# Keys, values and queries of one layer in half-array products, with another PSUM layout and batched sums

## The chip, the cores and the metric

The kernel runs on one core of a Trainium2 chip. The metric is device time in microseconds of one launch. Matrix products run on TensorE (PE in the profile, its weight loads PEld), elementwise work on VectorE (DVE), ScalarE (ACT) and GpSimd (POOL); SyncE (SP) issues the DMA transfers. Products are collected in PSUM, which the kernel lays out in banks of 512 float32 values per partition: four in the pool `ps_h` and two for each of the two tags of `ps_acc`.

## The reference

Four layers run one after the other on x of 2048 tokens by 576 channels: linear attention (A), MLP (B), attention again, MLP again. Layers 1 and 3 share their weights, and so do 2 and 4.

```python
def _A_ref(x, wqkv, wo):
    H = 32; Dh = D // H                       # 32 heads of 18
    q, k, v = ...                             # from x @ wqkv, 576 -> 3 * 576
    phi = lambda t: jnp.where(t > 0, t + 1, jnp.exp(t)) + 1e-6
    pq, pk = phi(q), phi(k)
    kv = jnp.einsum("bhsd,bhse->bhde", pk, v) # sum over all tokens
    z = jnp.einsum("bhsd->bhd", pk)
    num = jnp.einsum("bhqd,bhde->bhqe", pq, kv)
    den = jnp.einsum("bhqd,bhd->bhq", pq, z)[..., None] + 1e-6
    o = num / den
    return o... @ wo

def _B_ref(x, w1, b1, w2, b2):
    h = _gelu(layernorm(x) @ w1 + b1)         # 576 -> 4608
    return h @ w2 + b2

x = x + _A_ref(_layernorm(x), A_wqkv, A_wo)
x = x + _B_ref(_layernorm(x), ...)
x = x + _A_ref(_layernorm(x), A_wqkv, A_wo)   # Layer 3, the one that changes
x = x + _B_ref(_layernorm(x), ...)
```

## The kernel before

Tokens are cut into 16 tiles of 128 (`t`), and into four blocks of 512 (`c`). The normalized rows are held turned, as `yT`: channels on the partitions in five blocks of 128 (`KD`), tokens along the row. 576 channels are four and a half blocks, so the fifth block holds channels in its upper 64 partitions; the lower 64 partitions of the weights' fifth block are zero in `wqkv_sb`.

`layer_A` makes keys, values and queries. For each token tile `k_proj` (L443) makes two halves of 288 key columns, each of five products of the full array in one bank of the pool `ps_h` (four banks, tag "h"). `v_proj` (L456) makes two value parts of 252 and 324 columns in the two banks of `v_ps` (pool `ps_acc`, tag "accB"). From the third tile on, `q_proj` (L491) makes one group of up to 126 query columns for 512 tokens, five products of 512 columns, again in `ps_h`. The feature map phi is `phi_from_psum` (exponential and shifted copy on ACT, minimum and maximum on DVE) for queries and the first key half, and `phi_by_dve` (exponential on ACT; minimum L376 and a sum that reads PSUM, L378, on DVE) for the second key half. Values are copied to one of two tiles `v_ring`, four groups by ACT (L475) and the fifth by DVE (L480). `kv_acc(t - 1)` (L483) then adds the tile's five products into `kvacc` (pool `ps_acc`, tag "accA"), which stays open over all 16 tiles.

The order of PE's instructions is the order in which they are written: `pe` chains them. Each other engine runs its own instructions in the order in which they stand, and waits on semaphores. At the start of Layer 3 the layer norms of the last two row tiles are still under way: the residual sum of the last MLP tile (L427), the turning of rows (L230), statistics (L296 to L306), the power on POOL (L315) and the normalization (L334), all but the power on DVE. `pre_a1(t)` ticks that pipe once per tile. `land` brings a block of turned rows from DRAM to `yT` by two transfers, three for an MLP.

The MLP's first product (`m1_group`, L653) already works with half arrays: rows 0 to 63 and rows 64 to 127 of the array take separate products of 64 channels, with 4 or 5 products of 512 columns for each of four output blocks per half. The code lets the two halves take turns on a PSUM bank, and a relay stands between them: a tiny ACT copy (L699) that waits for the last product of one half and that the first product of the other half waits for.

After the last tile come `kvT`, the denominators, `kv_wo` and `wo_stage`, which use `ps_h` and both tags of `ps_acc`.

Of the kernel before, what the change touches and what calls it, by code (L numbers as in the profile page):

```python
# [15 lines left out]
P = 128  # L16
# [18 lines left out]
def build(tc, A_x, A_wqkv, A_wo, B_w1, B_b1, B_w2, B_b2, out, dbg=None, n_layers=4):  # L35
    nc = tc.nc
    dbg = dbg or {}
    with ExitStack() as ctx:
        const = ctx.enter_context(tc.tile_pool(name="const", bufs=1))
        ps_h = ctx.enter_context(tc.tile_pool(name="ps_h", bufs=4, space=PSUM))  # L40
        ps_acc = ctx.enter_context(tc.tile_pool(name="ps_acc", bufs=1, space=PSUM))
        dpool = ctx.enter_context(tc.tile_pool(name="dram", bufs=1, space=DRAM))

        x_in = A_x.flatten_outer_dims()
# [84 lines left out]
        relay_sb = const.tile([P, 2], F32, name="relay_sb")  # L129
        nc.gpsimd.memset(relay_sb[:], 0.0)  # L130
        chain = dict(last=None)

# [131 lines left out]
        class LNPipe:  # L264
            def __init__(self):
                self.items = []
# [94 lines left out]
            def drain(self):  # L361
                while self.items or landing:
                    self.tick()
# [9 lines left out]
        def phi_by_dve(ps_ap, out_ap, rows, n):  # L373
            e = work.tile([P, 512], BF16, name="phi_e", bufs=3)
            act_last["exp"] = nc.scalar.activation(out=e[0:rows, 0:n], in_=ps_ap, func=ACT.Exp).ins.name
            nc.vector.tensor_scalar(out=e[0:rows, 0:n], in0=e[0:rows, 0:n], scalar1=1.0, scalar2=1e-6,  # L376
                                    op0=ALU.min, op1=ALU.add)
            top = nc.vector.scalar_tensor_tensor(out=out_ap, in0=ps_ap, scalar=C1, in1=e[0:rows, 0:n],  # L378
                                                 op0=ALU.add, op1=ALU.max)
            dve_last["phi"] = top.ins.name  # L380

        def phi_from_psum(ps_ap, out_ap, rows, n, turned_cols=False):
            e = work.tile([P, 512], BF16, name="phi_e", bufs=3)
            a = work.tile([P, 512], BF16, name="phi_a", bufs=2)
            e_out, a_out = e[0:rows, 0:n], a[0:rows, 0:n]
            if turned_cols:
                e_out, a_out, ps_ap = spread(e_out), spread(a_out), gather(ps_ap)
            act_last["exp"] = nc.scalar.activation(out=e_out, in_=ps_ap, func=ACT.Exp).ins.name  # L388
            act_last["phi"] = nc.scalar.activation(out=a_out, in_=ps_ap, func=ACT.Identity, bias=C1,
                                                   scale=1.0).ins.name  # L390
            nc.vector.tensor_scalar(out=e[0:rows, 0:n], in0=e[0:rows, 0:n], scalar1=1.0, scalar2=1e-6,  # L391
                                    op0=ALU.min, op1=ALU.add)
            top = nc.vector.tensor_tensor(out=out_ap, in0=a[0:rows, 0:n], in1=e[0:rows, 0:n], op=ALU.max)
            dve_last["phi"] = top.ins.name
# [40 lines left out]
            return xn  # L435

        def layer_A(li, next_kind, pre_a1=None):
            kvacc = ps_acc.tile([P, 2, 512], F32, name="kvacc", tag="accA")
            pk_tiles = {}
            v_tiles = {}  # L440
            pq = {}
# [41 lines left out]
            def kv_acc(t):  # L483
                pk = pk_tiles.pop(t)
                va = v_tiles.pop(t)
                for g in range(G):
                    dst = kvacc[:, 0, GO[g]:GO[g] + GR[g]] if g < 4 else kvacc[:, 1, 0:GR[g]]
                    pe(nc.tensor.matmul(dst, lhsT=va[:, g, :], rhs=pk[:, GO[g]:GO[g] + GR[g]],  # L488
                                     start=(t == 0 and g in (0, 4)), stop=(t == NT - 1), skip_group_check=True))

            def q_proj(g, c):  # L491
# [5 lines left out]
                pq[(g, c)] = blk.tile([P, D], BF16, name="pq", tag="blk")  # L497
                phi_from_psum(qp[0:GR[g], :], pq[(g, c)][0:GR[g], 0:CA], GR[g], CA, turned_cols=(li > 0))

            q_left = [(g, c) for c in range(NCA) for g in range(G)]  # L500
            pe_chain["on"] = True
            for t in range(NT):
                if t != 1 or li > 0:
                    k_proj(t)
                if t == 0 and li == 0:
# [10 lines left out]
            q_proj(*q_left.pop(0))  # L516

            nc.vector.tensor_tensor(
                out=kvT[0:127, 0:4, :].rearrange("p g (h e) -> p g h e", h=7),
                in0=kvacc[0:127, 0, 0:504].rearrange("p (g h e) -> p g h e", g=4, h=7),  # L520
# [124 lines left out]
        class LayerB:  # L645
# [69 lines left out]

            def run(self):
                li, next_kind = self.li, self.next_kind

                def feed_next(c, i):
                    if c + 1 < NCB:  # L720
                        t = (c + 1) * TPC + i
                        lnp.feed(None, t, "B", "dve", "dma", load_from=t, after=dve_last["sum"])

                for c in range(NCB):
                    for g in range(self.done.get(c, 0), NGRP):
                        self.m1_group(c, g)
                        if g in (3, 5):
                            prefetch_xo(li, c * TPC + (g - 3) // 2, add_b2=True)
                        if g in (2, 3, 4, 5):
                            feed_next(c, g - 2)  # L730
                        lnp.tick(transposes=0)
                        lnp.tick(transposes=0)
                    self.flush()
                    if c == NCB - 1 and next_kind == "A":
                        warm_table(ACT.Exp, act_last["gelu"])
                    hT = self.hT.pop(c)
                    for j in range(TPC):
                        t = c * TPC + j
                        acc = ps_acc.tile([P, 2, 512], F32, name="m2_ps", tag=next_acc())
                        by_half = li == n_layers - 1 and t == NT - 1  # L740
                        steps = [(f, half) for half in range(2) for f in range(NF)] if by_half else \
                            [(f, half) for f in range(NF) for half in range(2)]
                        for f, half in steps:
                            pe(nc.tensor.matmul(acc[:, half, 0:HALF], lhsT=hT[f][:, j * P:(j + 1) * P],  # L744
                                                rhs=w2_sb[:, f, half * HALF:(half + 1) * HALF],
                                                start=(f == 0), stop=(f == NF - 1)))
# [113 lines left out]
```

## Time and profile before

| | |
|---|---|
| time, median of 3 runs (lowest to highest) | 777.58 us (777.58 to 777.61) |
| the profiled execution's own time | 777.09 us |
| its span | 775.4 us |
| PE busy | 765.1 us |
| DVE, ACT, POOL busy | 277.7, 335.1, 120.5 us |
| k_ps products of the full array (L449), Layers 1 and 3 | 320, 286 ns each |
| q_ps products (L494) | 200, 382 ns each |
| half-array products of 64x512 (L694) | 2592, 376 ns each |
| granted TensorE clock | 1.00 |

The duration of a product runs from its start to the end of its last write; products follow each other faster than that, since they are pipelined. In the profile `h_ps` and `hp_ps` are the two kinds of PSUM tile of the MLP's first product, `m_ps` that of its second, `w_sb` and `w_tail` its weights. Row tiles in DRAM are `x_d` and `y_d`.

### The profile page before, as it was taken

How to read it: one execution, taken by the hardware profiler on the slowest of the kernel's cores; microseconds unless marked ns; L12 is line 12 of the kernel's file. 1: busy time of each engine (PE TensorE's matmuls, PEld its weight loads, DVE VectorE, ACT ScalarE, POOL GpSimd, SP SyncE). 2: the span in 40 equal slices, each digit the busy share in tenths (PEclk: the TensorE clock that was granted, in tenths of full speed). 3: DMA queues.
4: the chain of work that ended last, by engine and by line, in shares of the span. 5: the costliest groups of instructions: out<-in, count | busy, mean ns of one | idle time of the engine just before them, and what ended most of it. 6: DMA issues, size and time to landing. Idle time of an engine off the chain costs nothing.

```text
span 775.4 us, 15774 instructions
## 1 busy us (share of the span) xinstructions
PE 765.1 (99%) x6613; PEld 495.0 (64%) x6613; DVE 277.7 (36%) x714; ACT 335.1 (43%) x734; POOL 120.5 (16%) x185
## 2 busy tenths in 40 slices
PE   8999999999999999999999999999999999999998
PEld 5776664675477457646777766547745764675476
DVE  7786964046013503401355579520140032000000
ACT  5888646404610650264046675561065026305600
POOL 4671322012000301200100004110030011001000
PEclk9999999999999999999999999999999999999999
DMA  8991474016301810320440006630141033011000
GB/s 254 267 299 46 137 253 103 18 50 173 88 16 48 199 50 32 92 64 17 138 107 1 1 2 210 248 82 8 32 129 52 16 124 80 8 32 54 1 11 21
DMA packets 73761, 69.10 MB, mean 89 GB/s; under 512 B 34266, under 2 KB 58330, under 8 KB 73690
## 3 DMA queue, kind: packets, MB, share of 16 engines
q1 hardware_dynamic: 73690, 68.10, 30.0%
q8 instruction: 51, 0.84, 0.5%
q14 instruction: 20, 0.16, 0.1%
HBM read 45.67 MB, written 22.41 MB: 88 GB/s over the span
## 4 chain that ended last, share of the span: by engine, by line
PE 94%; DVE 4%; issue 1%; ACT 1%; DMA 0%; POOL 0%; DVEq 0%; ACTq 0%
PE m_ps L744 37%; PE h_ps L694 20%; PE hp_ps L694 16%; PE q_ps L494 5%; PE k_ps L449 5%; PE wo_ps L589 4%; PE v_ps L470 3%; PE v_ps L462 2%; PE kvacc L488 1%; PE tp L352 1%; PE rden_ps L578 1%; PE warm_ps L176 1%; DVE rden L564 1%; DVE xo L427 0%; DMA x_d<-xo 0%
## 5 line engine op out<-in xcount | busy, mean ns | idle before, releaser
L744 PE MATMUL m_ps<-w_sb,hT 128*128 128x288 bf16 x2304 | 283.6, 286 | 0.0
L744 PEld LDWEIGHTS <-hT 128*128 128x128 bf16 x2304 | 224.8, 98 | 59.8 <-issue 3.4
L694 PEld LDWEIGHTS <-w_sb 64*128 64x128 bf16 x2304 | 124.5, 94 | 136.5 <-issue 1.9
L694 PE MATMUL hp_ps<-yT,w_sb 64*128 64x512 bf16 x1152 | 178.0, 376 | 0.0
L694 PE MATMUL h_ps<-yT,w_sb 64*128 64x512 bf16 x1152 | 148.0, 376 | 0.0
L699 ACT COPY relay_sb<-relay_sb 128x1 f32<-128x1 f32 x144 | 28.6, 198 | 264.5 <-PE h_ps L694 222.2
L315 POOL TENSOR_TENSOR ln_rstd<-ln_u,neg_half 128x1 f32<-128x1 f32 x64 | 36.8, 577 | 480.4 <-DVE ln_u L306 239.7
L690 ACT ACTIVATE hT<-h_ps,b1T 128x512 bf16<-128x512 f32 x144 | 91.2, 684 | 44.4 <-PE h_ps L694 44.4
L690 ACT ACTIVATE hT<-hp_ps,b1T 128x512 bf16<-128x512 f32 x144 | 91.2, 693 | 0.0
L427 DVE TENSOR_TENSOR xbf<-m_ps,xo 128x576 bf16<-128x576 f32 (+1 forms) x17 | 12.2, 722 | 219.9 <-PE m_ps L744 219.9
L427 DVE TENSOR_TENSOR xo<-m_ps,xo 128x576 f32<-128x576 f32 x16 | 12.1, 758 | 179.2 <-PE m_ps L744 179.2
L411 POOL TENSOR_TENSOR xo<-xo,b_bc 128x576 f32<-128x576 f32 x32 | 40.9, 1284 | 102.5 <-DMA xo<-x_d 62.7
L694 PE MATMUL h_ps<-yT,w_tail 64*128 64x512 bf16 x144 | 54.1, 376 | 0.0
L694 PE MATMUL hp_ps<-yT,w_tail 64*128 64x512 bf16 x144 | 54.1, 376 | 0.0
L494 PE MATMUL q_ps<-yT,wqkv_sb 128*126 128x512 bf16 (+1 forms) x200 | 50.0, 382 | 0.0
L589 PE MATMUL wo_ps<-kvwo,pq 126*128 126x288 bf16 (+1 forms) x320 | 43.9, 285 | 1.7 <-DVE pq L581 0.7
L449 PE MATMUL k_ps<-wqkv_sb,yT 128*128 128x288 bf16 x320 | 44.3, 286 | 0.0
L589 PEld LDWEIGHTS <-pq 126*128 126x128 bf16 (+1 forms) x320 | 30.2, 97 | 13.1 <-DVE pq L581 1.8
L449 PEld LDWEIGHTS <-yT 128*128 128x128 bf16 x320 | 31.0, 98 | 11.4
L694 PEld LDWEIGHTS <-w_tail 64*128 64x128 bf16 x288 | 27.1, 94 | 17.1
L388 ACT ACTIVATE phi_e<-k_ps 128x288 bf16<-128x288 f32 x46 | 19.3, 419 | 34.6 <-PE k_ps L449 33.6
L391 DVE TENSOR_SCALAR phi_e<-phi_e 128x288 bf16<-128x288 bf16 (+2 forms) x86 | 25.1, 292 | 24.6 <-ACT phi_e L388 24.5
(100 smaller groups left out, 633.2 us busy)
## 6 DMA issues: line engine op xcount, KB each, us to landing
xo<-x_d SPq DMA_DIRECT2D x48, 288.0 KB, 3.6
x_d<-xo SPq DMA_DIRECT2D x32, 288.0 KB, 2.1
xl<-x_d SPq DMA_DIRECT2D x24, 288.0 KB, 4.6
y_d<-turned SPq DMA_DIRECT2D x40, 144.0 KB, 3.2
w_sb<-in_B_w_dram SPq DMA_DIRECT2D x6, 864.0 KB, 9.5
yT<-y_d SPq DMA_DIRECT2D x10, 512.0 KB, 4.1
w_sb<-in_B_w_dram SPq DMA_DIRECT2D x9, 512.0 KB, 5.6
x_d<-xn SPq DMA_DIRECT2D x16, 288.0 KB, 2.2
```

Source lines behind the costliest of these rows:

```text
L315: nc.gpsimd.tensor_tensor(out=rstd[:], in0=it["u"][:], in1=neg_half[:], op=ALU.pow)
L391: nc.vector.tensor_scalar(out=e[0:rows, 0:n], in0=e[0:rows, 0:n], scalar1=1.0, scalar2=1e-6, op0=ALU.min, op1=ALU.add)
L411: nc.gpsimd.tensor_tensor(out=xo[:], in0=xo[:], in1=b2_bc[:], op=ALU.add)
L427: total = nc.vector.tensor_tensor(out=xn[:, cols].rearrange("p (h n) -> p h n", h=nh), in0=ps, in1=xo[:, cols].rearrange("p (h n) -> p h n ...
L449: pe(nc.tensor.matmul(kp[:, 0:HALF], lhsT=yT[:, k, tok], rhs=wqkv_sb[:, k, D + half * HALF: D + (half + 1) * HALF], start=(k == 0), stop=( ...
L470: pe(nc.tensor.matmul(vp[:, 1, 0:324], lhsT=yT[:, k, tok], rhs=wqkv_sb[:, k, 2 * D + 252: 3 * D], start=(k == 0), stop=(k == KD - 1)))
L494: pe(nc.tensor.matmul(qp[0:GR[g], :], lhsT=wqkv_sb[:, k, GO[g]:GO[g] + GR[g]], rhs=yT[:, k, c * CA:(c + 1) * CA], start=(k == 0), stop=(k ...
L589: pe(nc.tensor.matmul(wp[:, half, 0:HALF], lhsT=pq[(g, c)][0:GR[g], j * P:(j + 1) * P], rhs=kvwo[g][0:GR[g], half * HALF:(half + 1) * HALF ...
L690: act_last["gelu"] = nc.scalar.activation(out=to, in_=ps, func=ACT.Gelu_apprx_tanh, bias=b1T[:, f:f + 1], scale=1.0).ins.name
L694: mm = pe(nc.tensor.matmul(dst[n], lhsT=wt, rhs=mv, start=(seen[n] == 0), stop=(seen[n] == 8)))
L699: relay = nc.scalar.copy(out=relay_sb[:, 1:2], in_=relay_sb[:, 0:1])
L744: pe(nc.tensor.matmul(acc[:, half, 0:HALF], lhsT=hT[f][:, j * P:(j + 1) * P], rhs=w2_sb[:, f, half * HALF:(half + 1) * HALF], start=(f == ...
```

## The change

Layer 3 (`li > 0`) gets a loop of its own; Layer 1 keeps the old one.

Each value part, key half and query group becomes a job (`half_jobs`, `q_job`) of 64-row products: four for each half of the array, and one more for one of them (`tail`), which takes the last 64 channels. `RowTiles` writes the order. Jobs enter the upper half as they come; a job enters the lower half when two later ones have been added. Products are written in the order in which two counters of columns say that they would start. Between a job's last upper product and its first lower one stands a relay, here a POOL memset on `relay_sb`. So that keys and values may take their tail in the lower half, the last 64 rows of the weights are loaded a second time to partitions 64 to 127 (one transfer, at the start of the MLP before), and `land` loads the last 64 channels of `yT` to both halves for Layer 3 too.

The jobs of a tile stand in the order query, values, keys, where the old loop had keys, values, sums, query. Both key halves go by `phi_by_dve`. The PSUM pool `ps_acc` is closed at the start of the layer, and two new ones take its place: `v_banks` with two single banks for the value parts, and `ps_kv` for `kvacc`. Behind `kvT` they are closed and `ps_acc` is opened again. The sums of four tiles are written together, after tiles 4, 8 and 12 and at the end, with the full array; for that the value ring grows to five tiles by the three `y_ring` tiles, each prepared by three POOL memsets. The pipe of layer norms is ticked twice per tile.

```diff
-        ps_acc = ctx.enter_context(tc.tile_pool(name="ps_acc", bufs=1, space=PSUM))
+        psum_pools = ctx.enter_context(ExitStack())
+        ps_acc = psum_pools.enter_context(tc.tile_pool(name="ps_acc", bufs=1, space=PSUM))
...
-                for hi in range(2 if kind == "B" else 1):
+                for hi in range(2):
...
+                def v_start(half):
+                    def start():
+                        tiles[half] = v_banks.tile([P, 512], F32, name="v_ps", tag="v")[:, 0:edges[half + 1] - edges[half]]
...
+                def v_finish(half):
+                    def finish():
+                        nc.scalar.copy(out=va[:, 2 * half:2 * half + 2, 0:126],
+                                       in_=tiles[half][:, 0:252].rearrange("p (g c) -> p g c", g=2))
+                        if half == 1:
+                            nc.vector.tensor_copy(out=va[:, 4, 0:72], in_=tiles[1][:, 252:324])
...
+                def k_finish(half):
+                    def finish():
+                        phi_by_dve(tiles["k", half], tiles["pk"][:, half * HALF:(half + 1) * HALF], P, HALF)
...
+                for half in range(2):
+                    cols = slice(2 * D + edges[half], 2 * D + edges[half + 1])
+                    jobs.append(dict(w=y_of, m=rows_of(cols), tail=1, n=edges[half + 1] - edges[half],
+                                     start=v_start(half), finish=v_finish(half)))
+                for half in range(2):
+                    cols = slice(D + half * HALF, D + (half + 1) * HALF)
+                    jobs.append(dict(w=y_of, m=rows_of(cols), tail=1 - half, n=HALF,
+                                     start=k_start(half), finish=k_finish(half)))
...
+            class RowTiles:
...
+                def emit(self, op, first, last):
+                    job, hi, w, m = op
+                    mm = pe(nc.tensor.matmul(job["dst"], lhsT=w, rhs=m, start=(first and hi == 0), stop=(last and hi == 1)))
+                    self.at[hi] += job["n"]
+                    if first and hi == 1:
+                        tc.add_manual_dep(mm.ins, job["relay"], SYNC, reason="row tiles take turns on a PSUM bank")
+                    if last and hi == 0:
+                        relay = nc.gpsimd.memset(relay_sb[:, 2:3], 0.0)
+                        tc.add_manual_dep(relay.ins, mm.ins.name, SYNC, reason="row tiles take turns on a PSUM bank")
+                        job["relay"] = self.relay = relay.ins.name
+                    if last and hi == 1:
+                        job["finish"]()
+
+                def lower(self, limit):
+                    while self.low and (limit is None or self.at[1] <= limit):
+                        self.emit(*self.low.pop(0))
...
+                def add(self, job):
+                    if len(self.begun) == 2:
+                        if not self.low:
+                            self.at[1] = max(self.at)
+                        self.queue_lower(self.begun.pop(0))
+                    self.begun.append(job)
+                    job["dst"] = job["start"]()
+                    ops = self.ops(job, 0)
+                    for i, op in enumerate(ops):
+                        self.lower(self.at[0] - 1)
+                        self.emit(op, i == 0, i == len(ops) - 1)
+
+                def full(self, func):
+                    func()
+                    self.at = [max(self.at)] * 2
...
+            if li > 0:
+                va_ring = v_ring + [y[:].rearrange("p (g c) -> p g c", g=G) for y in
+                                    (y_ring[(state["ycnt"] + i) % NY] for i in range(NY))]
+                psum_pools.close()
+                v_banks = psum_pools.enter_context(tc.tile_pool(name="v_banks", bufs=2, space=PSUM))
+                ps_acc = psum_pools.enter_context(tc.tile_pool(name="ps_kv", bufs=1, space=PSUM))
+                stream = RowTiles()
+                for t in range(NT):
+                    pre_a1(t)
+                    pre_a1(t)
+                    if t in (2, 3, 4):
...
+                    if t >= 2:
+                        stream.add(q_job(*q_left.pop(0)))
+                    for job in half_jobs(t):
+                        stream.add(job)
+                    if t % 4 == 0 and t > 0:
+                        stream.full(lambda: [kv_acc(u) for u in range(t - 4, t)])
+                stream.drain()
+                for u in range(NT - 4, NT - 1):
+                    kv_acc(u)
...
+            if li > 0:
+                psum_pools.close()
+                ps_acc = psum_pools.enter_context(tc.tile_pool(name="ps_acc", bufs=1, space=PSUM))
...
+                if next_kind == "A":
+                    nc.sync.dma_start(out=wqkv_sb[64:P, 4, D:3 * D], in_=A_wqkv[4 * P:D, D:3 * D])
```

More of the change, by code (lines that the diff above doesn't have):

```diff
@@ L128, in build @@
         SYNC = mybir.DependencyInfo(mybir.DependencyClass.Sync, mybir.DependencyReason.DATA)
-        relay_sb = const.tile([P, 2], F32, name="relay_sb")
+        relay_sb = const.tile([P, 4], F32, name="relay_sb")
         nc.gpsimd.memset(relay_sb[:], 0.0)
@@ L437, in layer_A @@
         def layer_A(li, next_kind, pre_a1=None):
-            kvacc = ps_acc.tile([P, 2, 512], F32, name="kvacc", tag="accA")
+            nonlocal ps_acc
+            kvacc_of = {}
             pk_tiles = {}
@@ L485, in kv_acc @@
                 va = v_tiles.pop(t)
+                if t == 0:
+                    kvacc_of["ps"] = ps_acc.tile([P, 2, 512], F32, name="kvacc", tag="accA")
+                kvacc = kvacc_of["ps"]
                 for g in range(G):
@@ L498, in q_proj, with half_jobs, k_start, start @@
                 phi_from_psum(qp[0:GR[g], :], pq[(g, c)][0:GR[g], 0:CA], GR[g], CA, turned_cols=(li > 0))
+            def half_jobs(t):
+                tok = slice(t * P, (t + 1) * P)
+                tiles = {}
+                va = va_ring[t % len(va_ring)]
+                edges = (0, 252, D)
+                def v_start(half):
+                    def start():
+                        tiles[half] = v_banks.tile([P, 512], F32, name="v_ps", tag="v")[:, 0:edges[half + 1] - edges[half]]
+                        return tiles[half]
+                    return start
+                def v_finish(half):
[4 more added lines that the diff above has]
+                            nc.vector.tensor_copy(out=va[:, 4, 0:72], in_=tiles[1][:, 252:324])
+                            v_tiles[t] = va
+                    return finish
+                def k_start(half):
+                    def start():
+                        tiles["k", half] = ps_h.tile([P, 512], F32, name="k_ps", tag="h")[:, 0:HALF]
+                        if half == 0:
+                            tiles["pk"] = blk.tile([P, D], BF16, name="pk", tag="blk")
+                        return tiles["k", half]
+                    return start
+                def k_finish(half):
+                    def finish():
+                        phi_by_dve(tiles["k", half], tiles["pk"][:, half * HALF:(half + 1) * HALF], P, HALF)
+                        if half == 1:
+                            pk_tiles[t] = tiles["pk"]
+                    return finish
+                def rows_of(cols):
+                    return lambda r, k: wqkv_sb[r, k, cols]
+                y_of = lambda r, k: yT[r, k, tok]
+                jobs = []
+                for half in range(2):
[6 more added lines that the diff above has]
+                                     start=k_start(half), finish=k_finish(half)))
+                return jobs
@@ new lines, in q_job, with start, finish @@
+            def q_job(g, c):
+                hold = {}
+                def start():
+                    hold["q"] = ps_h.tile([P, 512], F32, name="q_ps", tag="h")[0:GR[g], :]
+                    return hold["q"]
+                def finish():
+                    pq[(g, c)] = blk.tile([P, D], BF16, name="pq", tag="blk")
+                    phi_from_psum(hold["q"], pq[(g, c)][0:GR[g], 0:CA], GR[g], CA, turned_cols=True)
+                return dict(w=lambda r, k: wqkv_sb[r, k, GO[g]:GO[g] + GR[g]],
+                            m=lambda r, k: yT[r, k, c * CA:(c + 1) * CA], tail=0, n=CA, start=start, finish=finish)
@@ new lines, in layer_A, with __init__, ops, queue_lower @@
+            class RowTiles:
+                def __init__(self):
+                    self.at = [0, 0]
+                    self.begun = []
+                    self.low = []
+                def ops(self, job, hi):
+                    r = slice(64 * hi, 64 * hi + 64)
+                    return [(job, hi, job["w"](r, k), job["m"](r, k))
+                            for k in range(KD - 1 + (job["tail"] == hi))]
+                def emit(self, op, first, last):
[13 more added lines that the diff above has]
+                        self.emit(*self.low.pop(0))
+                def queue_lower(self, job):
+                    ops = self.ops(job, 1)
+                    self.low += [(op, i == 0, i == len(ops) - 1) for i, op in enumerate(ops)]
+                def add(self, job):
[12 more added lines that the diff above has]
+                    self.at = [max(self.at)] * 2
+                def drain(self):
+                    while self.begun:
+                        self.queue_lower(self.begun.pop(0))
+                    self.lower(None)
@@ L500, in layer_A @@
             q_left = [(g, c) for c in range(NCA) for g in range(G)]
             pe_chain["on"] = True
-            for t in range(NT):
-                if t != 1 or li > 0:
+            if li > 0:
[9 more added lines that the diff above has]
+                    if t in (2, 3, 4):
+                        assert not lnp.busy()
+                        va = va_ring[t]
+                        for part, value in ((va[:, 4, 72:126], 0.0), (va[:, :, 126:127], 1.0), (va[:, :, 127:128], 0.0)):
+                            init = nc.gpsimd.memset(part, value)
+                            tc.add_manual_dep(init.ins, stream.relay, NOSYNC, reason="relays first")
+                    if t >= 2:
[7 more added lines that the diff above has]
+                    kv_acc(u)
@@ L504, in layer_A @@
+            for t in range(NT if li == 0 else 0):
+                if t != 1:
                     k_proj(t)
-                if t == 0 and li == 0:
+                if t == 0:
                     phi0["dve"] = dve_last["phi"]
@@ L516, in layer_A @@
             q_proj(*q_left.pop(0))
+            kvacc = kvacc_of["ps"]
             nc.vector.tensor_tensor(
```

## The prediction

> **What bounds the kernel now.** I read the page first, then one stretch of Layer 3 in the order of time. The page says that TensorE is the bound almost everywhere, and the windows say it of this stage too.
>
> ```profile
> span 775.4 us, 15774 instructions
> ...
> PE 94%; DVE 4%; issue 1%; ACT 1%; DMA 0%; POOL 0%; DVEq 0%; ACTq 0%
> ...
> 391.30:451.90 60.60, 60.51 (x480) 45.42 (x478) 34.07 (x117) 39.71 (x93) 0.55 (x1) 1.00 0.12 31
> ```
>
> The last row (window, its length, busy time of PE, weight loads, DVE, ACT, POOL, granted clock) is the stage that changes: PE is busy for 60.51 of 60.60 us, DVE for 34, ACT for 40, POOL for 0.55. So columns saved here are time saved, as long as nothing else starts to make PE wait.
>
> One tile in the steady part, from the timeline:
>
> ```profile
> 442.58 1.39 PE L449 MATMUL k_ps<-wqkv_sb,yT 128*128 128x288 bf16 x10
> ...
> 444.33 0.44 ACT L375 ACTIVATE phi_e<-k_ps 128x288 bf16<-128x288 f32 x1
> ...
> 444.81 0.23 DVE L376 TENSOR_SCALAR phi_e<-phi_e 128x288 bf16<-128x288 bf16 x1
> ...
> 445.08 0.46 DVE L378 SCALAR_TENSOR_TENSOR pk<-k_ps,phi_e 128x288 bf16<-128x288 f32 x1
> ...
> 446.39 1.39 PE L449 MATMUL k_ps<-wqkv_sb,yT 128*128 128x288 bf16 x10
> ```
>
> A tile takes 446.39 - 442.58 = 3.81 us. The middle rows are the way out of a key bank: exponential 0.44, minimum 0.23, sum 0.46, with about 0.04 between.
>
> The entry into the stage:
>
> ```profile
> 391.42 1.39 PE L449 MATMUL k_ps<-wqkv_sb,yT 128*128 128x288 bf16 x10
> 391.62 0.76 DVE L427 TENSOR_TENSOR xo<-m_ps,xo 128x576 f32<-128x576 f32 x1 [4.94 <-PE m_ps L744]
> ...
> 392.30 0.77 DVE L230 STREAM_TRANSPOSE turned<-y_ring 128x576 bf16<-128x576 bf16 x1
> ```
>
> and the same DVE chain one row tile earlier, with nothing between its links:
>
> ```profile
> 383.47 0.77 DVE L230 STREAM_TRANSPOSE turned<-y_ring 128x576 bf16<-128x576 bf16 x1
> ...
> 386.10 0.58 DVE L334 TENSOR_SCALAR y_ring<-xo,ln_mv,ln_rstd 128x576 bf16<-128x576 f32 x1 [0.73 <-POOL ln_rstd L315]
> ```
>
> PE goes straight from the last m_ps product into keys, because k_ps lies in other banks than the m_ps that DVE still adds at 391.62.
>
> Half-array products as the MLP runs them, and its way back to the full array:
>
> ```profile
> 492.69 0.38 PE L694 MATMUL h_ps<-yT,w_tail 64*128 64x512 bf16 x1
> ...
> 494.63 0.38 PE L694 MATMUL h_ps<-yT,w_tail 64*128 64x512 bf16 x1
> ...
> 524.63 0.38 PE L694 MATMUL hp_ps<-yT,w_tail 64*128 64x512 bf16 x1
> ...
> 524.94 1.28 PE L744 MATMUL m_ps<-w_sb,hT 128*128 128x288 bf16 x9
> ```
>
> Nine steps of two halves take 1.94 us, 0.216 per step of 512 columns; a full product of 288 takes 0.1225 (95 in 11.80 us at 379.78). The slope is 0.417 us per 1000 columns, the constant 2.5 ns per product.
>
> **The change, part by part.** I count from the first product at 391.42 to the last tile's kvacc at 451.29: 59.87 us now. Behind that point the order is the old one.
>
> *Columns.* Now: 16 tiles x 10 x 288 for keys and values and 14 queries x 2560, 128,000 columns, 53.33 us, 390 products x 2.5 ns = 0.98; 15 kvacc groups at 0.26 (396.35 to 396.61) are 3.93, one more query 1.08; the remaining 0.55 are small waits in tiles 0 to 2. After: the upper row runs 2304 columns (both value halves of tile 0) before the lower may begin, then the lower has 16 x 2592 + 16 x 2880 + 28,672 = 116,224, which includes two keys halves alone at the end; the code's own counters lose 572 more where they are set equal. 119,100 columns, 49.62 us, plus 360 x 2.5 ns = 0.90: 50.52. The kvacc groups (now by fours) and the full query stay, 3.93 and 1.08.
>
> *The first value bank, +1.01.* `psum_pools.close()` puts the value banks where m_ps was, and values now come first. In the built order the first product waits for the add at L427, done at 392.38; with 0.05 to PE (DVE pq at 478.97, PE at 479.02) it starts at 392.43, not 391.42. All of PE is queued behind it.
>
> *The second value bank, +1.60.* The second values product of tile 1 waits for the small DVE copy out of tile 0's bank. DVE's order puts the rest of the last layer norm ahead of it: turn 392.30, norm 2.63 later (383.47 to 386.10) at 394.93, turn 0.64 later (395.66 to 396.30), copy 0.69 after that at 396.26, 0.23 long, PE at 396.54. PE gets there after 5904 columns and 21 products, 2.51 us from 392.43, at 394.94. Before, the copy stood between the links of the norm (L480 at 394.85) and cost no such wait.
>
> *Switches, +0.67.* Full to half and back: 524.63 + 0.216 = 524.85, next at 524.94, 0.095 lost. Three batches cost two each, the end one; the one at entry lies in the first hole. In the middle of the stream both rows must run empty; I keep 0.095 and bound it from above by 0.3 each (+1.4).
>
> *Key banks, +3.0.* A key bank is used again four allocations later: the second key half of tile t+1 takes the first one's bank of tile t. The way out, from the time the next product could start: 0.16 (0.286 less 0.122), 0.03, 0.44, 0.04, 0.23, 0.04, 0.46, 0.05: 1.45 us. The time there is: for tile 7 the counters put the lower half's end at column 57,472 and the next use at 60,560, 1.29 us plus 0.03 for products. The lower row has 7520 columns a tile with a query, the upper 7456, so the lag grows: 1.44 at tile 2, 1.32 at 7, 1.02 at 13. Missing: 0.01, 0.03, 0.05, 0.08, 0.11, 0.13, 0.19, 0.21, 0.24, 0.27, 0.40, 0.43, 0.45, in all 2.6; the query that takes the second half's bank finds it some 0.03 later still, 0.4 for 13. Not below 0; not over 4.5 if every hand-over costs 0.01 to 0.02 more, eight to a tile.
>
> *At nothing.* 78 POOL memsets as relays: 0.10 each (relay_sb, L130) on an engine with 0.55 us of work here; POOL's queue holds them behind the 0.55 rstd once, inside the 1.60. The tightest, the query's, needs 0.16 + 0.03 + 0.10 + 0.05 and a weight load of 0.09, 0.43, and has 0.48. The nine memsets of the borrowed y_ring tiles (0.12 to 0.14) stand behind a relay with a query of 1.07 to follow. Five more transfers on SP: four yT tails (0.52 of queue each, 4.1 to land; the last is needed at tile 12, over 30 us later) and wqkv's 144 KB, issued some 280 us ahead of its use. ACT loses one 0.43 pass a tile and gets a second small copy, DVE trades 0.54 for 0.69; both have a third of the tile free.
>
> Sum: 1.01 + 50.52 + 3.93 + 1.08 + 1.60 + 0.67 + 3.0 = 61.81 against 59.87, **+1.9 us**. The profiled execution has 777.09, its span 775.4, the median is 777.58, so 779.5 on the median.
>
> **Rivals.**
>
> *The key banks are ready* (not slower). The extra 3.0 rests on differences of 0.01 to 0.45 us. If the lower row lags less on the chip than in the counters, so that the 1.45 us fit, the sum is -1.1: 776.5. For: ACT and DVE are two thirds busy at most, and the gap is 1.44 when queries begin. Against: the lag grows in the written order, which PE keeps. If the copy at 396.26 also came 0.8 earlier, 775.7.
>
> *Unlike lengths do not overlap.* The MLP pairs 512 with 512; here 512 runs beside 252, 288 and 324. If rows went in step, each pair as long as its longer half, a tile would take 8784 columns for 7520, 0.53 us x 14 = +7.4, and the key banks would have their time (-3.0): 783.9. Against it: weight loads of both rows start together a full step ahead in the MLP. The Trainium skill (PSUM — Partial Sum Buffer, Engine vs sequencer instructions) says that matmuls start and complete in program order; no run here shows it for two rows of unlike length, and taken strictly the rule would make this rival the forecast.
>
> *DVE and POOL hold each other up.*
>
> ```profile
> 497.15 1.28 POOL L411 TENSOR_TENSOR xo<-xo,b_bc 128x576 f32<-128x576 f32 x1
> 497.22 1.53 DVE L334 TENSOR_SCALAR y_ring<-xl,ln_mv,ln_rstd 128x576 bf16<-128x576 f32 x1 [0.67 <-POOL ln_rstd L315]
> ```
>
> The norm that took 0.58 takes 1.53 beside a POOL instruction. A memset of 0.10 in front of the minimum in each of 13 tiles' way out adds 1.3: 780.8. The Trainium skill (SBUF — State Buffer, Who interferes with whom) calls the port that the two share an exclusive lock for the whole instruction; the two rows agree.
>
> That halves do not run side by side at all would cost over 40 us; the MLP's 0.216 per pair excludes it.
>
> **How the numbers follow.** A difference under 0.2% (1.56 us, 776.0 to 779.1) is what I call no change. Forecast 0.52, its own range 778.2 to 781.5 (key banks 1.7 to 4.5 and part of the switches); banks ready 0.20; unlike lengths 0.14; ports 0.12; the rest 0.02. Faster by more than 0.2%: a third of the second, 0.08. Within: the rest of the second and a third of the forecast, 0.32. Slower: 0.60. The range goes from the banks-ready sum to the unlike lengths' one, 776.5 to 784.0.
>
> **What would show it.** Right: first v_ps product about 1.0 us after the last m_ps; a PE wait on the DVE copy of about 1.6 near 394.9; k_ps waits on pk that grow from tile 3 to 15; about 0.1 around each kvacc batch; tile period 3.3 to 3.6. Wrong: a period of 3.2 with no k_ps wait (first rival), 288- and 512-column halves starting in step (second), minimum rows of 0.3 (third), or waits on relay_sb of more than 0.1 per tile.

## The result, and the profile after

The changed kernel takes 779.04 us (median of 14 runs, 778.85 to 779.94), the one before 777.56 (14 runs, 777.15 to 778.07): the ratio is 1.0022, with a 95% interval of 1.0014 to 1.0029. So it is a little slower, 1.48 us. The interval leaves 1 out, so the direction is clear; the size lies just inside the 0.2% that the prediction called no change (up to 779.1).

The page of the changed kernel, its span, the chain of waits by engine, and the window from the moment the last m_ps product gives way (0.12 after its start) to the start of the last tile's kvacc (columns: window, length, busy time of PE, weight loads, DVE, ACT, POOL, granted clock, DMA share, GB/s):

```profile
span 777.4 us, 16544 instructions
...
PE 93%; DVE 3%; ACT 1%; DMA 1%; issue 1%; POOL 0%; DVEq 0%; ACTq 0%; POOLq 0%
...
391.94:453.30 61.36, 59.49 (x784) 48.88 (x783) 38.41 (x116) 38.42 (x92) 9.88 (x88) 1.00 0.12 32
```

The stage was 59.87 us and is 61.36: 1.49 more, which is the whole difference of the medians. (The stage begins 0.52 later in this one execution than in the one of before; that offset was already there at the first MLP product, 110 us in. Behind the stage both executions need the same, 324.1 us.) PE still reads as busy for 59.49 of 61.36. That is the trap of this profile: a half product of 288 columns starts every 0.12 us and is drawn 0.28 long (the profile models where a product ends), so a pause of 0.1 to 0.2 between starts is covered by the bars, and the view of PE's waits in this stage lists only two lines:

```profile
PE v_ps L584 <- DVE v_ring L522: 1.0, 1, 1.0
PE v_ps L584 <- DVE xo L428: 0.8, 1, 0.8
```

The entry, all engines, shows both:

```profile
392.14 0.76 DVE L428 TENSOR_TENSOR xo<-m_ps,xo 128x576 f32<-128x576 f32 x1 [4.94 <-PE m_ps L899]
...
392.96 1.19 PE L584 MATMUL v_ps<-wqkv_sb,yT 64*128 64x252 bf16 x10 [0.85 <-DVE xo L428]
...
395.39 0.58 DVE L335 TENSOR_SCALAR y_ring<-xo,ln_mv,ln_rstd 128x576 bf16<-128x576 f32 x1 [0.67 <-POOL relay_sb L589]
...
396.00 0.78 DVE L231 STREAM_TRANSPOSE turned<-y_ring 128x576 bf16<-128x576 bf16 x1
396.70 0.20 DVE L522 CAST v_ring<-v_ps 128x72 bf16<-128x72 f32 x1
396.95 0.29 PE L584 MATMUL v_ps<-wqkv_sb,yT 64*128 64x324 bf16 x1 [0.96 <-DVE v_ring L522]
```

The last m_ps product starts at 391.82 and gives way at 391.94; the first half product starts at 392.96, behind the residual sum, 1.02 later. From there PE needs 2.51 us by the prediction's count to the second values product of tile 1, so it was due at 395.47; it starts at 396.95, behind the value copy that stands third in DVE's queue, after the layer norm's apply and the turn: 1.48.

Now one tile near the end, where the small waits are:

```profile
447.12 0.28 PE L584 MATMUL k_ps<-wqkv_sb,yT 64*128 64x288 bf16 x1
447.17 0.58 PE L584 MATMUL v_ps<-wqkv_sb,yT 64*128 64x252 bf16 x2
447.18 0.23 DVE L522 CAST y_ring<-v_ps 128x72 bf16<-128x72 f32 x1 [0.18 <-ACT y_ring L519]
...
447.47 0.29 PE L584 MATMUL k_ps<-wqkv_sb,yT 64*128 64x288 bf16 x1
...
448.22 0.46 DVE L379 SCALAR_TENSOR_TENSOR pk<-k_ps,phi_e 128x288 bf16<-128x288 f32 x1
...
448.73 0.28 PE L584 MATMUL k_ps<-wqkv_sb,yT 64*128 64x288 bf16 x1
```

The value copy ends at 447.41. The product that waits for its bank, the first of the second values half in the upper row, starts at 447.46; the view draws it in one line with the product of 252 columns at 447.17, after which the row was free at 447.28. The lower row is held up with it: its next product, written behind the waiting one, starts at 447.47, though the one before had started at 447.12 and one takes 0.12. The keys sum ends at 448.68, and the next keys half starts at 448.73. I laid every start of the 702 half products beside the written order in this way (a product is late when it starts after its own row's columns, and after the product issued before it, would have allowed). From tile 3 on the late starts of jobs in the upper row add up to 2.68 us: 1.15 behind the keys sums of the first half, 0.30 for queries, and 1.23 behind value copies. They grow from some 0.03 a wait at tile 6 to 0.24 at tile 15.

A batch of kvacc, with the change to the full array and back:

```profile
422.23 0.28 PE L584 MATMUL k_ps<-wqkv_sb,yT 64*128 64x288 bf16 x1
422.44 0.43 PE L493 MATMUL kvacc<-pk,y_ring 128*128 128x126 bf16 x5
...
423.23 0.42 PE L493 MATMUL kvacc<-pk,y_ring 128*128 128x126 bf16 x5
423.58 0.43 PE L584 MATMUL q_ps<-yT,wqkv_sb 64*126 64x512 bf16 x1
```

422.23 plus 0.12 is 422.35, the first sum starts at 422.44: 0.09. Twenty sums of 0.0525 end at 423.49, the query starts at 423.58: 0.09 again. The query's second product comes another 0.05 later than its row's columns ask for (423.85 instead of 423.80); that is not in the sums below.

So 4.34 us of PE work are saved (59.87 less the 55.53 of columns, sums and the full query) and 5.85 are paid back: 1.02 + 1.48 + 2.68 + 0.67. The 0.67 is the forecast's, seven changes at 0.095, which the 0.09 of this batch supports.

### The profile page after: what moved, and what is told of

It reads as the page before. It is cut to its first block, busy times and chain, and to the rows that moved or that the text cites. A ratio compares the mean times of both kernels' runs of the same rounds, so it can differ in the third digit from the quotient of the medians.

```text
span 777.4 us, 16544 instructions
## 1 busy us (share of the span) xinstructions
PE 764.1 (98%) x6920; PEld 498.9 (64%) x6925; DVE 283.1 (36%) x714; ACT 334.2 (43%) x734; POOL 129.4 (17%) x272
## 4 chain that ended last, share of the span: by engine, by line
PE 93%; DVE 3%; ACT 1%; DMA 1%; issue 1%; POOL 0%; DVEq 0%; ACTq 0%; POOLq 0%
PE m_ps L899 36%; PE h_ps L847 20%; PE hp_ps L847 16%; PE wo_ps L742 4%; PE q_ps L499 3%; PE k_ps L451 2%; PE v_ps L584 2%; PE k_ps L584 2%; PE q_ps L584 2%; PE v_ps L472 1%; PE kvacc L493 1%; PE v_ps L464 1%; PE tp L353 1%; PE rden_ps L731 1%; DVE rden L717 1%
## 5 line engine op out<-in xcount | busy, mean ns | idle before, releaser
L584 PEld LDWEIGHTS <-yT 64*128 64x128 bf16 x576 | 39.4, 94 | 10.2 <-issue 3.9
L584 PE MATMUL v_ps<-wqkv_sb,yT 64*128 64x252 bf16 (+1 forms) x288 | 42.3, 283 | 1.9 <-DVE v_ring L522 1.0
L584 PE MATMUL k_ps<-wqkv_sb,yT 64*128 64x288 bf16 x288 | 41.7, 283 | 0.0
L389 ACT ACTIVATE phi_e<-q_ps 126x512 bf16<-126x512 f32 (+1 forms) x40 | 23.9, 598 | 20.3 <-PE q_ps L499 13.5
L499 PE MATMUL q_ps<-yT,wqkv_sb 128*126 128x512 bf16 (+1 forms) x130 | 32.5, 382 | 0.0
```

What stands on the lines that cost most here:

```text
L499: pe(nc.tensor.matmul(qp[0:GR[g], :], lhsT=wqkv_sb[:, k, GO[g]:GO[g] + GR[g]], rhs=yT[:, k, c * CA:(c + 1) * CA], start=(k == 0), stop=(k ...
L584: mm = pe(nc.tensor.matmul(job["dst"], lhsT=w, rhs=m, start=(first and hi == 0), stop=(last and hi == 1)))
```

## The experiments

The theory to be tested: the half products do what they should, and the saving is lost to three things, the two entry waits and a lag. The lower row has more columns than the upper one, so it falls behind from tile to tile, and each PSUM bank is given back later against the time when the upper row wants it. The rivals: the late starts are a price of each hand-over, or of rows of unlike length, whatever the lag; and a wait that is taken away only moves on. All ratios below are to the kernel before, run beside them. Its median was 777.56, 777.48 and 777.14 us in the three groups of runs (the changed kernel's; tails_even, values_before_norm, sums_every_tile and keys_first_even; the other four), so a difference between medians of two groups can be off by some 0.4; where that matters, the difference in the stage's length in the traces stands beside it.

**The lag taken away (tails_even).** A keys half has nine half products; which row makes the ninth is free.

```diff
+                FLIP = (4, 8, 12)
...
-                    jobs.append(dict(w=y_of, m=rows_of(cols), tail=1 - half, n=HALF,
+                    jobs.append(dict(w=y_of, m=rows_of(cols), tail=0 if t in FLIP else 1 - half, n=HALF,
```

> The ninth half product of the first keys half goes to the upper row in tiles 4, 8 and 12 (everything else as in the changed kernel), so the lower row no longer falls further behind. Theory (the growing lag makes the bank waits of tiles 3 to 15, 2.7 us): by the code's column counters the gap of a key bank is then 1.39 us or more in every tile, where it fell to 0.97, and that of a value bank 0.94, where it fell to 0.55; waits fall from 2.7 to about 0.5, 264 columns less are 0.1: 776.7 on the median, 779.0 for the changed kernel. Rival (the waits are a price of each hand-over, or of rows of unlike length, whatever the lag): only the 0.1 of the columns, 778.9.

Measured: 776.74 us, ratio 0.9990 (0.9981 to 0.9998): 2.3 less than the changed kernel (2.5 by the stage, 58.89), by moving three products out of some 700 from one row to the other. The late starts from tile 3 on fall from 2.68 to some 0.1, none above 0.016, and the two entry waits stay as they were (1.0 and 0.8 in the view of waits). The hand-overs and the unlike lengths are all still there, so neither is the cause. The same trace tells of rows of unlike length; its PE in tiles 14 and 15:

```profile
444.24 0.37 PE L585 MATMUL q_ps<-yT,wqkv_sb 64*126 64x512 bf16 x1
...
444.45 0.38 PE L585 MATMUL q_ps<-yT,wqkv_sb 64*126 64x512 bf16 x1
...
444.92 0.28 PE L585 MATMUL k_ps<-wqkv_sb,yT 64*128 64x288 bf16 x1
444.99 0.27 PE L585 MATMUL v_ps<-wqkv_sb,yT 64*128 64x252 bf16 x1
445.04 0.28 PE L585 MATMUL k_ps<-wqkv_sb,yT 64*128 64x288 bf16 x1
445.10 0.27 PE L585 MATMUL v_ps<-wqkv_sb,yT 64*128 64x252 bf16 x1
```

Halves of 512 columns start every 0.21, of 288 every 0.12 and of 252 every 0.11, each at its row's own rate beside the other (the query's products at 444.24 and 444.45 run beside keys products that start at 444.31, 444.43 and 444.55).

**The second value bank (values_before_norm).** The copy of tile 0 goes ahead of the layer norm's apply on DVE, and the turn behind a keys sum; one tick of the norm's pipe a tile, and the borrowed y_ring buffers start one later, so that they are free.

```diff
+            if dve_last.get("cast") is not None:
+                tc.add_manual_dep(turn.ins, dve_last["phi"], NOSYNC, reason="rows are turned behind the keys")
...
+                            if dve_last.get("cast") is not None:
+                                tc.add_manual_dep(norm.ins, dve_last["cast"], NOSYNC, reason="values first")
```

> On DVE the small value copy of tile 0 stands ahead of the last layer norm's apply, and that row's turn behind the first keys' sum; the products are the same. Theory (the second value bank waits for that copy, 1.5 us, and nothing else is late there): the copy ends about 395.9 and not 396.9, PE goes on 1.0 earlier, 778.0. Rival (the wait is only moved: the query of tile 2 then waits for keys sums of tile 0 that now stand behind the apply): 0.3 at most, 778.7.

Measured: 778.23 us, ratio 1.0012 (1.0003 to 1.0021), 0.8 less than the changed kernel (0.7 by the stage, 60.69). DVE and PE in this run:

```profile
395.11 0.23 DVE L526 CAST v_ring<-v_ps 128x72 bf16<-128x72 f32 x1 [0.95 <-ACT v_ring L523]
...
401.18 0.77 DVE L231 STREAM_TRANSPOSE turned<-y_ring 128x576 bf16<-128x576 bf16 x1
401.88 0.19 DVE L526 CAST y_ring<-v_ps 128x72 bf16<-128x72 f32 x1
...
402.12 0.29 PE L589 MATMUL v_ps<-wqkv_sb,yT 64*128 64x324 bf16 x1
```

The copy is out at 395.34 and PE goes on at 395.40, 4.01 after the last m_ps product where the changed kernel needed 5.01. But the turn has moved to 401.18 and stands there ahead of the copy of tile 2: PE waits 0.35 at 402.12. So 1.00 of the 1.48 was DVE's order, as forecast; 0.48 of it stayed. A third of what was won came back, at another value copy and not at the query that the rival named.

**The price of a change of mode (sums_every_tile, every_tile_even).** First kvacc after every tile:

```diff
-                    if t % 4 == 0 and t > 0:
-                        stream.full(lambda: [kv_acc(u) for u in range(t - 4, t)])
+                    if t >= 2:
+                        stream.full(lambda: kv_acc(t - 2))
```

> kvacc is summed after every tile and not by fours: 14 batches in the stream where there were 3, so 22 more changes between half and full array; the kvacc products are the same 75. Theory: 22 x 0.095 is 2.1 more, but every tile now gives its banks 0.45 more (five kvacc products and two changes), which is more than any bank wait of the changed kernel: of its 2.7 about 2.4 go. Sum -0.3, 778.7, and no wait on pk or value copies from tile 4 on. Rival (in the middle of the stream both rows must run empty, 0.3 a change, my upper bound): 6.6 - 2.4, 783.2. Second rival (bank waits do not depend on the time between two uses): 2.1 more, 781.1.

Measured: 790.26 us, ratio 1.0163 (1.0149 to 1.0177), 11.2 slower than the changed kernel. All three readings were wrong. One tile of it:

```profile
447.38 0.23 DVE L522 CAST y_ring<-v_ps 128x72 bf16<-128x72 f32 x1 [0.67 <-ACT y_ring L519]
...
447.67 0.29 PE L584 MATMUL v_ps<-wqkv_sb,yT 64*128 64x324 bf16 x1 [0.36 <-DVE y_ring L522]
...
448.86 0.46 DVE L379 SCALAR_TENSOR_TENSOR pk<-k_ps,phi_e 128x288 bf16<-128x288 f32 x1
...
449.37 0.28 PE L584 MATMUL k_ps<-wqkv_sb,yT 64*128 64x288 bf16 x1 [0.36 <-DVE pk L379]
```

These are the bank waits again, now 0.53 and 0.66 a tile. My error was to think that a batch lies between two uses of a bank and gives it time. In the written order the first keys half's lower products run after the batch and the next tile's second half ahead of the next one: nothing is gained. And at each batch the rows meet with the lower one behind, and the program's counters are set to the later of the two: the lag grows by that step 14 times and not 3. By the counters a key bank's gap falls to 0.71 us by tile 9, a value bank's to 0.29. That is one more reading after the fact, so it got a run of its own: the same sums after every tile, with `FLIP = range(3, 16, 2)`.

> Sums after every tile as in sums_every_tile, and besides the ninth half product of the first keys half in the upper row in tiles 3, 5, 7, 9, 11, 13 and 15. Theory (the 11 us that sums_every_tile lost are bank waits: at every batch the rows meet again with the lower row behind, and the counters' gap of a key bank fell to 0.71 us, that of a value bank to 0.29): with the tails moved the gaps stay at 1.49 and 0.95, the waits go, and against the changed kernel there remain 22 changes of mode at 0.095 (+2.1), 692 columns (+0.3) and the 2.4 us of its own bank waits that go here too: 779.0. Rival (a change in the middle of the stream is dear, 0.4 to 0.5 us each): the waits are not touched by the tails, 788 to 790.

Measured: 779.34 us, ratio 1.0027 (1.0017 to 1.0036). Seven products moved to the other row take 10.9 us off. The bank waits after tile 2 are gone, and against tails_even, which has none either, it is 2.6 slower by the medians and 2.9 by the stage: 22 changes of mode and 956 more columns (0.4), so 0.10 to 0.115 a change. That is more than the 0.09 seen on either side of a batch, and the 0.03 to 0.05 by which the query's second product comes late behind 13 of the 14 batches here can account for it.

**Key banks or value banks (keys_out_early).** The first keys half leaves PSUM by two ACT passes, as it did before the change.

```diff
-                        phi_by_dve(tiles["k", half], tiles["pk"][:, half * HALF:(half + 1) * HALF], P, HALF)
+                        phi = phi_by_dve if half == 1 else phi_from_psum
+                        phi(tiles["k", half], tiles["pk"][:, half * HALF:(half + 1) * HALF], P, HALF)
```

> The first keys half leaves its bank by two ACT passes, as in the kernel before, and DVE makes the sum from SBUF; products, order and tails are the changed kernel's. Its bank is free after some 1.1 us and not 1.45. First reading (my prediction's: all of the bank waits stand on key banks): 2.6 go, 776.4. Second reading (value banks stand right behind, 1.2 of the 2.7 in the trace): the 1.1 on the first half's bank goes, but the value banks' waits grow, since the lag is the same, and the second half's exponential now stands 0.4 later on ACT, so queries wait more: 0.4 at most is won, 778.6.

Measured: 778.25 us, ratio 1.0013 (1.0005 to 1.0022), 0.8 less than the changed kernel by the medians, 0.6 by the stage (60.77). Late starts behind the first keys half: none. Behind value copies: 1.22, hardly less than before, up to 0.30 a wait; for queries 0.8 where it was 0.3. Of the 2.6 of the first reading a quarter came; the second reading holds in the main, though it was the queries' waits that grew and not the value banks': freeing one kind of bank leaves the others where the lag has put them.

**The entry turned round (keys_first_even).**

```diff
-                    if t >= 2:
-                        stream.add(q_job(*q_left.pop(0)))
-                    for job in half_jobs(t):
-                        stream.add(job)
+                    jobs = half_jobs(t)
+                    jobs = jobs[2:] + ([q_job(*q_left.pop(0))] if t >= 1 else []) + jobs[:2]
+                    for job in jobs:
+                        stream.add(job)
```

(besides the tails of tiles 0, 1, 4, 8 and 12, and the full query ahead of the last kvacc in layer 1 only)

> Each tile runs keys, query, values (the changed kernel: query, values, keys); a query as half products in tiles 1 to 15, and none as a full product ahead of the last kvacc; the ninth half product of the first keys half in the upper row in tiles 0, 1, 4, 8 and 12. Theory: the first product finds its key bank free (-1.0), the second values bank of tile 1 comes some 2.4 us later than the changed kernel's and finds the copy done (-1.5), bank waits fall from 2.7 to about 0.5 (-2.2), columns and products +0.25: 774.6, 0.4% faster than the kernel before. Rival (removed entry waits come back as waits on keys sums, which DVE makes behind the layer norm): half of the 2.5 comes back, 775.9. Rival (bank waits have another cause than the lag): 776.8.

Measured: 776.56 us, ratio 0.9989 (0.9980 to 0.9998): faster than before, but 2 us short of the forecast. Its entry:

```profile
394.44 0.55 POOL L316 TENSOR_TENSOR ln_rstd<-ln_u,neg_half 128x1 f32<-128x1 f32 x1 [0.71 <-DVE ln_u L307]
394.93 0.25 POOL L590 MEMSET relay_sb<- 128x1 f32 x2
...
395.09 0.31 PE L585 MATMUL v_ps<-wqkv_sb,yT 64*128 64x324 bf16 x1 [0.30 <-POOL relay_sb L590]
...
395.66 0.77 DVE L231 STREAM_TRANSPOSE turned<-y_ring 128x576 bf16<-128x576 bf16 x1
396.35 0.42 DVE L379 SCALAR_TENSOR_TENSOR pk<-k_ps,phi_e 128x288 bf16<-128x288 f32 x1
...
396.82 0.37 PE L585 MATMUL q_ps<-yT,wqkv_sb 64*126 64x512 bf16 x1 [0.88 <-DVE pk L379]
```

The first wait is gone (keys start right behind m_ps), but the same layer norm now holds up something else: a relay stands behind its rstd on POOL (PE 0.58 late at 395.09), and the keys sum stands behind its turn on DVE (1.18 late at 396.82, not 0.88: the bar before it hides 0.3). Here the rival "it comes back" won, with 1.76 of the 2.5 where it had named half; the other 0.2 is bank waits of 0.7 from tile 3 on where 0.5 was expected.

**The layer norm put off (keys_first_gated, keys_first_act).** The norm has time: its rows are needed some 30 us later. So its pipe is not ticked in tile 0, and its power, its apply and its turn are put later on their engines (the turn also behind the value copy before it, and the borrowed y_ring buffers start one later):

```diff
+            if dve_last.get("gate") is not None:
+                tc.add_manual_dep(turn.ins, dve_last["phi"], NOSYNC, reason="keys first")
...
+                        if dve_last.get("gate") is not None:
+                            tc.add_manual_dep(power.ins, dve_last["gate"], NOSYNC, reason="relays first")
...
+                            if dve_last.get("gate") is not None:
+                                tc.add_manual_dep(norm.ins, dve_last["phi"], NOSYNC, reason="keys first")
...
+                    if t > 0:
+                        dve_last["gate"] = stream.relay
+                        pre_a1(t)
+                        pre_a1(t)
```

> keys_first_even with another order at the entry on DVE and POOL: the last layer norm's rstd (POOL) behind the relay of tile 0's second values half, its apply and its turn (DVE) behind the first sums of tile 1. Theory (the 1.2 us of the query of tile 1 and the 0.6 of a relay in keys_first_even come from that layer norm alone): both go, some 0.3 comes back where the apply and the turn now stand ahead of a value copy: 775.1. Rival (the wait only moves on to the next bank): 0.3 better at most, 776.3.

Measured: 775.49 us, ratio 0.9977 (0.9967 to 0.9987). Both waits are gone, and 0.44 comes back, at the second value bank in tile 2: the copy out of it, at 400.88, stands on DVE behind the turn of 399.48 and a query's minimum and maximum (0.3 was expected). With the small value copy on ACT (`nc.scalar.copy` for `nc.vector.tensor_copy`) besides:

> keys_first_gated with the small value copy on ACT and not on DVE, so nothing of the way out of a value bank stands in DVE's queue. Theory: a value bank is free some 0.1 sooner (no hand-over from ACT to DVE, 0.2 for the copy either way), and the copies of tiles 0 to 2 do not stand behind the layer norm: 774.8. Rival (ACT's queue, with 0.2 more per tile, makes the exponentials later, and key banks wait for it): 775.8.

Measured: 774.97 us, ratio 0.9970 (0.9958 to 0.9982), the lowest median of all. The late starts behind value copies are gone (0.65 in keys_first_gated); those of keys and queries grow from 0.43 to 0.59. Its entry, PE and DVE:

```profile
391.43 1.15 PE L593 MATMUL k_ps<-wqkv_sb,yT 64*128 64x288 bf16 x8
...
394.04 0.46 DVE L387 SCALAR_TENSOR_TENSOR pk<-k_ps,phi_e 128x288 bf16<-128x288 f32 x1
...
394.88 0.38 PE L593 MATMUL q_ps<-yT,wqkv_sb 64*126 64x512 bf16 x1
...
397.70 0.57 DVE L341 TENSOR_SCALAR y_ring<-xo,ln_mv,ln_rstd 128x576 bf16<-128x576 f32 x1
```

The first half product starts 0.1 after the last m_ps product gives way (391.34), the keys sum is out at 394.50, 0.4 ahead of the query that needs its bank, and the apply comes at 397.70. The stage takes 57.18 us, 4.2 less than in the changed kernel and 2.7 less than before.

## Why the prediction was right

Forecast were 779.5 us and slower; it is 779.04 and slower, by a little less than the 0.2% under which the prediction spoke of no change. To that band it had given 0.32, to more than that 0.60. By its own steps:

- *Columns, sums, full query: 55.53.* What is left of the 61.36 when the measured waits and changes of mode are taken out is 55.51. This term decided the size of everything else, and it closes to about 0.1: the 0.05 behind each of three batches is not taken out.
- *The first value bank, 1.01.* Measured 1.02, behind the sum named. Keys-first runs have no such wait.
- *The second value bank, 1.60.* Measured 1.48. The chain was right link by link; values_before_norm showed that 1.00 of it is DVE's order. It did not show that the cost is free to take away: a third of what was won there came back, and in keys_first_even 1.76 of 2.5.
- *Switches, 0.67.* The batch in the trace shows 0.09 on both sides, every_tile_even 0.10 to 0.115 over 22 more of them. The upper bound of 0.3 was not needed.
- *Key banks, 3.0.* Measured 2.68 with the growth from tile 3 to 15 that was forecast, and tails_even showed that the lag is its cause. But the step named the wrong banks for almost half of it: 1.23 of the 2.68 stand on value banks, and the waits behind first keys halves, forecast at 2.6, are 1.15. The way out of a key bank was well sized (1.45; the first halves' banks that are waited for show 1.42 to 1.43 up to tile 13 and 1.50 in tiles 14 and 15). I worked it out against its gap and did not do it for a value bank, whose gap in the same counters falls from 1.13 to 0.55 us, while ACT's pass, DVE's copy and their hand-overs need some 0.9 (0.88 to 0.97 in the waits of the second values half). The two share one lag, and PE held up for one bank gives time to the other, as keys_out_early shows from the other side. That the total still came out close was luck: waits that were left out stood in for waits that were named too large.
- *At nothing: relays.* Right but for the one that stands behind the rstd (0.23 at 395.45, inside the 1.48). From tile 3 on relays are late by 0.03 at most.
- *Rivals.* "Key banks are ready" fails by the 2.68; tails_even, 776.74, is where it would have been (it said 776.5). "Unlike lengths do not overlap" is refuted by the starts in the trace; there was no run with equal lengths. The Trainium skill's rule (PSUM — Partial Sum Buffer, Engine vs sequencer instructions), that matmuls start and complete in program order, does not keep the two rows in step here: halves of 252 start every 0.11 us beside halves of 288 every 0.12. Nor do the starts of the two rows always keep the written order in this trace: the lower row's first product is written behind the upper row's eighth, and it starts at 393.76, the eighth at 393.80. "DVE and POOL hold each other up" fails too: the minimum of keys (L377) takes 0.22 to 0.24 in all of this stage, beside a memset or not.

The sum was 0.45 too high: 0.12 for the second value bank and 0.32 for the banks of the later tiles.

## What to carry to other kernels

When work is dealt to two halves of an engine that run on their own, count which half gets more, and how the difference adds up: 64 columns a tile, and a step at each batch of sums, were next to nothing in the sum of work and 2.7 us in waits, since every buffer's free time shrank with them. Move an odd piece to the other half now and then before looking for faster ways out of the buffers. And where a wait is on a queue's order, move the late-needed work far back, not just one place: put one place back, it held up the next thing.

## Of the hardware, not expected

- A pause of PE between half products is not seen in busy time nor in the view of waits below some 0.3 us, because a product of 0.12 is drawn 0.28 long. 2.7 us of loss were to be found only in the starts.
- What DVE and POOL cost each other showed the other way round: of the 78 relay memsets 65 took 0.10 us, and the 13 longer ones (0.11 to 0.24) all ran beside a minimum on DVE (eleven a query's, two a keys half's), while no minimum was longer beside a memset. In each of the 13 the minimum had begun 0.09 to 0.19 us before the memset, and the memset ended 0.04 after it; in three more the minimum had begun only 0.02 to 0.03 before, and the memset took its 0.10. The Trainium skill (SBUF — State Buffer, Who interferes with whom) calls the port that the two share an exclusive lock for the whole instruction, held by the one that issues first. The 13 rows agree: the short POOL instruction came second and waited.
